# One more tile transposed by DMA, one more reciprocal broadcast by way of DRAM, and late weights issued by GpSimd, in a fused attention and gated-MLP kernel

## The chip, the cores and the metric

One core of one Trainium2 chip. The metric is the device time of one execution in microseconds (us), median of several runs; lower is better. TensorE is called PE, VectorE DVE, ScalarE ACT, GpSimd POOL and SyncE SP.

## The reference

x is 1 x 2048 x 512 in bf16. Two branches work on the layer-normalized x, and their product is added to x:

```python
# A: 32 heads of 16, each position looks at 8 positions, 2 apart, back from itself
q, k, v = split(xn @ wqkv)
logits  = einsum("bhsd,bhswd->bhsw", q, kg) * Dh**-0.5     # kg, vg: k, v gathered at s, s-2, ..., s-14
attn    = softmax(where(mask, logits, -1e9))
s       = einsum("bhsw,bhswd->bhsd", attn, vg) @ wo
# B: gated MLP, 512 -> 1792 -> 512
h = gelu(xn @ w_gate) * (xn @ w_up)
g = silu(h @ w_down)
return x + s * g          # xn = layernorm(x)
```

## The kernel before

It works through the 2048 positions in four chunks of 512 (four tiles of 128 each). For each chunk: 14 "glu" steps (gate and up matmuls, gelu, product), then the q, k and v projections of the next chunk ("qkv"), then 4 "down" steps (w_down, wo, output). The attention of a chunk is laid between these by a table: `at((stage, chunk, step), function, ...)` runs a function ahead of that step. The order of instructions is the order of the program. What the change and the argument touch (cuts are marked):

```python
def load_late_weights():                       # w_down and wo, 5 DMAs on SP's queue
    nc.sync.dma_start(out=wd_sb[:], in_=B_w_down.rearrange("(k p) n -> p k n", p=P))
    for g in range(NC):
        nc.sync.dma_start(out=wo_sb[:, g, :], in_=...)

def moments(t):                                # statistics on DVE, the power -0.5 on POOL
    ...
    nc.gpsimd.tensor_tensor(out=rstd[:, t, :], in0=rstd[:, t, :], in1=mhalf[:], op=ALU.pow)

def transpose(t, parts=1, copy=None):          # 4 PE transposes into a PSUM tile and a copy out of it
    ...
def transpose_by_dma(t):                       # 4 DMA transposes on SP's queue
    ...
def spread_reciprocals(j):                     # 1/denominator to all rows by 4 PE matmuls ("sp_ps") and an ACT copy
    ...
def spread_by_dma(j):                          # the same: stored to DRAM (rs_d), read back four times (rb)
    ...
def av_sums(j):                                # 32 matmuls over the eight products "pv": "o_ps"
    ...
def divide(j):                                 # oT = o_ps * rb, two DVE instructions of 2 groups each
    ...

at(("glu", 0, 7 + i), moments, 2 * TPQ + i)    # i = 0..3: tiles 8 to 11
at(("glu", 0, 8 + i), normalize, 2 * TPQ + i)  # DVE: needs the power
at(("glu", 0, 9), logits, 0)                   # and seven small memsets of E on POOL
...
at(("qkv", 1, 10), av_sums, 0)
at(("glu", 3, 12), spread_reciprocals, 3)      # the last chunk only; the others by DMA
at(("glu", 3, 13), divide, 3)
at(("glu", 0, 0), load_late_weights)
```

The softmax here doesn't subtract the row's maximum and nothing guards it: scores larger than these inputs give would overflow.

## Time and profile before

| | before |
|---|---|
| time, first three runs | 230.54, 231.28 and one of 339.7 us; median 231.28 |
| time, 11 runs of a later session | median 230.46 us (230.14 to 230.93) |
| span in the profile | 228.8 us, mean granted PE clock 1.0 |
| PE busy | 222.7 us, 97% |
| DVE, ACT, POOL busy | 65%, 57%, 10% |
| transfers | mean 106 GB/s |

PE is the bound. A row of a timeline in the profile begins with the start in us, then the length, engine, line, operation, what it writes and reads, and how many instructions stand together; in brackets is how long the engine sat idle before it, and what released it. Ends on PE overlap the next start (the transposes at 22.14 are listed with 0.39 us, and the next group starts at 22.36), so I go by starts.

### The profile page before, as it was taken

How to read it: one execution, taken by the hardware profiler on the slowest of the kernel's cores; microseconds unless marked ns; L12 is line 12 of the kernel's file. 1: busy time of each engine (PE TensorE's matmuls, PEld its weight loads, DVE VectorE, ACT ScalarE, POOL GpSimd, SP SyncE). 2: the span in 40 equal slices, each digit the busy share in tenths (PEclk: the TensorE clock that was granted, in tenths of full speed). 3: DMA queues.
4: the chain of work that ended last, by engine and by line, in shares of the span. 5: the costliest groups of instructions: out<-in, count | busy, mean ns of one | idle time of the engine just before them, and what ended most of it. 6: DMA issues, size and time to landing. Idle time of an engine off the chain costs nothing.

```text
span 228.8 us, 3516 instructions
## 1 busy us (share of the span) xinstructions
PE 222.7 (97%) x1303; PEld 106.8 (47%) x1323; DVE 147.6 (65%) x234; ACT 130.6 (57%) x215; POOL 21.7 (10%) x61
## 2 busy tenths in 40 slices
PE   7999999999999999999999999999999999999994
PEld 5865444444444444444444444444444444444453
DVE  4593996894898198865678169735449429845232
ACT  3679779764514867476721687646741387647211
POOL 1048944100000000110000000000000000000000
PEclk9999999999999999999999999999999999999999
DMA  6999599922366611110266711110038910000001
GB/s 157 357 375 376 140 175 199 315 98 80 91 153 152 135 23 29 27 29 0 92 162 152 162 29 23 26 34 6 30 104 193 202 30 3 0 0 4 23 23 46
DMA packets 29857, 24.33 MB, mean 106 GB/s; under 512 B 9488, under 2 KB 29840, under 8 KB 29840
## 3 DMA queue, kind: packets, MB, share of 16 engines
q1 hardware_dynamic: 29840, 24.11, 41.0%
q8 instruction: 10, 0.16, 0.3%
q14 instruction: 7, 0.06, 0.1%
HBM read 18.61 MB, written 4.31 MB: 100 GB/s over the span
## 4 chain that ended last, share of the span: by engine, by line
PE 94%; ACT 2%; DVE 1%; DMA 1%; issue 1%; ACTq 0%; DVEq 0%
PE y_ps L411 21%; PE u_ps L242 21%; PE g_ps L242 20%; PE qkv_ps L242 17%; PE s_ps L421 6%; PE L_ps L299 3%; PE o_ps L370 3%; DMA x_sb<-in_A_x_dram 1%; PE q_ps L242 1%; PE tr L208 1%; DVE stats L177 1%; ACT L395 1%; ACT u L397 1%; PE den_ps L319 0%; ACT xnT L217 0%
## 5 line engine op out<-in xcount | busy, mean ns | idle before, releaser
L242 PE MATMUL u_ps<-xnT,wu_sb 128*128 128x512 bf16 x223 | 57.3, 379 | 0.2
L242 PE MATMUL g_ps<-xnT,wg_sb 128*128 128x512 bf16 x214 | 56.5, 379 | 0.6 <-issue 0.2
L411 PE MATMUL y_ps<-wd_sb,h 128*128 128x512 bf16 (+1 forms) x234 | 50.9, 366 | 0.2
L399 DVE TENSOR_TENSOR h<-ge,u 128x512 bf16<-128x512 bf16 x56 | 23.8, 424 | 37.5 <-ACT u L397 36.8
L288 DVE TENSOR_TENSOR pk<-q_sb,k_sb 128x2048 bf16<-128x2048 bf16 x32 | 37.8, 1221 | 7.0 <-ACT k_sb L263 7.0
L395 ACT ACTIVATE ge<-g_ps 128x512 bf16<-128x512 f32 x56 | 33.6, 600 | 14.7 <-PE g_ps L242 14.0
L397 ACT ACTIVATE u<-u_ps 128x512 bf16<-128x512 f32 x56 | 33.6, 599 | 14.6 <-PE u_ps L242 14.4
L242 PE MATMUL qkv_ps<-xnT,wqkv_sb 128*128 128x512 bf16 (+1 forms) x203 | 40.5, 354 | 0.2
L356 DVE TENSOR_TENSOR pv<-E,v_arr 128x2048 bf16<-128x2048 bf16 x32 | 38.6, 1217 | 0.0
L411 PEld LDWEIGHTS <-h 128*128 128x128 bf16 x238 | 23.3, 98 | 25.3
L418 ACT ACTIVATE sl<-y_ps 128x512 bf16<-128x512 f32 (+1 forms) x17 | 9.7, 573 | 44.0 <-PE y_ps L411 44.0
L242 PEld LDWEIGHTS <-wu_sb 128*128 128x128 bf16 x224 | 21.9, 98 | 26.6 <-issue 0.3
L242 PEld LDWEIGHTS <-wg_sb 128*128 128x128 bf16 x224 | 21.2, 98 | 26.8 <-issue 3.0
L242 PEld LDWEIGHTS <-wqkv_sb 128*128 128x128 bf16 x224 | 21.7, 98 | 19.6 <-issue 0.4
L429 DVE TENSOR_TENSOR m<-s_ps,sl 128x512 bf16<-128x512 f32 (+1 forms) x17 | 11.2, 658 | 22.4 <-PE s_ps L421 22.4
L421 PE MATMUL s_ps<-wo_sb,oT 128*128 128x512 bf16 (+1 forms) x68 | 16.6, 366 | 0.0
L193 POOL TENSOR_TENSOR rstd<-rstd,mhalf 128x1 f32<-128x1 f32 x12 | 7.7, 638 | 78.9 <-DVE rstd L190 76.7
L266 ACT ACTIVATE vst<-qkv_ps 128x512 bf16<-128x512 f32 x16 | 9.6, 598 | 6.4 <-PE qkv_ps L242 6.4
L263 ACT ACTIVATE k_sb<-qkv_ps 128x512 bf16<-128x512 f32 (+1 forms) x20 | 10.2, 517 | 3.4 <-PE qkv_ps L242 3.2
L260 ACT ACTIVATE q_sb<-qkv_ps 128x512 bf16<-128x512 f32 (+1 forms) x16 | 8.7, 545 | 3.5 <-PE qkv_ps L242 3.3
L421 PEld LDWEIGHTS <-oT 128*128 128x128 bf16 x68 | 6.6, 98 | 7.2
L382 DVE TENSOR_TENSOR oT<-o_ps,rbd 128x1024 bf16<-128x1024 f32 x6 | 7.1, 1219 | 3.7 <-PE qkv_ps L242 3.7
(52 smaller groups left out, 119.3 us busy)
## 6 DMA issues: line engine op xcount, KB each, us to landing
v_arr<-vT SPq DMA_DIRECT2D x16, 520.0 KB, 5.1
vT<-vst SPq DMA_DIRECT2D x16, 128.0 KB, 2.8
out_dram<-o_t SPq DMA_DIRECT2D x15, 128.0 KB, 2.3
wg_sb<-in_B_w_gate_dram SPq DMA_DIRECT2D x2, 896.0 KB, 10.8
wu_sb<-in_B_w_up_dram SPq DMA_DIRECT2D x2, 896.0 KB, 10.9
wd_sb<-in_B_w_down_dram SPq DMA_DIRECT2D x1, 1792.0 KB, 16.9
wqkv_sb<-in_A_wqkv_dram SPq DMA_DIRECT2D x3, 512.0 KB
x_sb<-in_A_x_dram SPq DMA_DIRECT2D x3, 512.0 KB, 11.6
```

Source lines behind the costliest of these rows:

```text
L242: nc.tensor.matmul(ps, lhsT=w[:, dk, lo : lo + P], rhs=xnT[j][:, dk, i0 : i0 + n], start=(dk == 0), stop=(dk == NC - 1),)
L263: nc.scalar.activation(out=k_sb[:, c, lo : lo + n], in_=ps, func=AF.Copy)
L266: nc.scalar.activation(out=vst[:], in_=ps, func=AF.Copy)
L288: nc.vector.tensor_tensor(out=pk[:], in0=st[j]["q"][:], in1=k_sb[:, :, off : off + TQ], op=ALU.mult)
L356: nc.vector.tensor_tensor(out=pv[:], in0=st[j]["E"][:, wh, :].unsqueeze(1).to_broadcast([P, 4, TQ]), in1=st[j]["va"][:, 4 * g : 4 * g + 4, ...
L395: nc.scalar.activation(out=ge[:], in_=g_ps[:], func=AF.Gelu_apprx_tanh)
L397: nc.scalar.activation(out=u[:], in_=u_ps[:], func=AF.Copy)
L399: nc.vector.tensor_tensor(out=h[:], in0=ge[:], in1=u[:], op=ALU.mult)
L411: nc.tensor.matmul(y[:], lhsT=st[j][fc][:, tt * P : (tt + 1) * P], rhs=wd_sb[:, fc, cols], start=(fc == 0), stop=(fc == NF - 1),)
L418: nc.scalar.activation(out=sl[:, cols], in_=y[:], func=AF.Silu)
L421: nc.tensor.matmul(s[:], lhsT=st[j]["oT"][:, g, tt * P : (tt + 1) * P], rhs=wo_sb[:, g, cols], start=(g == 0), stop=(g == NC - 1),)
L429: nc.vector.tensor_tensor(out=m[:], in0=s[:], in1=sl[:, cols], op=ALU.mult)
```

## The change

The intent: PE is the bound, so take four transposes (tile 6) and four spread matmuls (last chunk) off it and let DMAs do the work; take the late weights out of SP's queue, where they now would stand behind more transposes; and bring the first q weights forward. Tile 7 was transposed by DMA before as well; its transposes now stand behind those of tile 6 and behind load_v (the v_arr loads) on SP's queue.

```diff
-    for t in range(TPQ):
+    for t in range(TPQ - 1):
         load_x(t)
-    for i in range(3):
+    load_w(wqkv_sb, A_wqkv, 0, D)
+    load_x(TPQ - 1)
+    for i in range(1, 3):
         load_w(wqkv_sb, A_wqkv, i * D, (i + 1) * D)
...
     def load_late_weights():
-        nc.sync.dma_start(out=wd_sb[:], ...
+        nc.gpsimd.dma_start(out=wd_sb[:], ...
         for g in range(NC):
-            nc.sync.dma_start(
+            nc.gpsimd.dma_start(
...
-        nc.gpsimd.memset(spread[:], 0.0)          # and the 16 copies that fill "spread"
...
-        xn = xns[t] = sm4.tile([P, D], BF16, name="xn")     # 4 buffers, shared with vst and o_t
+        xn = xns[t] = xnp.tile([P, D], BF16, name="xn")     # 6 buffers of its own
...
-        if i < TPQ - 1:
+        if i < 2:
             at(("glu", 0, i), transpose, TPQ + i)
...
-        if j + 1 < NJ:
-            at(("glu", j, 11), spread_by_dma, j)
-            at(("qkv", j + 1, 6), divide, j)
-        else:
-            at(("glu", j, 12), spread_reciprocals, j)       # the PE form is gone
-            at(("glu", j, 13), divide, j)
+        at(("glu", j, 11), spread_reciprocals, j)           # now the DMA form
+        at(("qkv", j + 1, 6) if j + 1 < NJ else ("down", j, 0), divide, j)
...
     warm_up(17, TQ // 2)
+    warm_up(4, P)
...
-    at(("glu", 0, 0), transpose_by_dma, 2 * TPQ - 1)
+    at(("glu", 0, 0), transpose_by_dma, TPQ + 2)
     at(("glu", 0, 0), load_v, 0)
-    at(("glu", 0, 0), load_late_weights)
+    at(("glu", 0, 0), transpose_by_dma, TPQ + 3)
+    at(("glu", 0, 9), load_late_weights)
```

More of the change, by code (lines that the diff above doesn't have):

```diff
@@ L68 @@
     sm4 = pool("sm4", 4)
+    xnp = pool("xnp", 6)
     dram = pool("dram", 1, space=bass.MemoryType.DRAM)
@@ L80 @@
     vT = dram.tile([D, SV], BF16, name="vT")
-    rs_d = [dram.tile([P, P], BF16, name=f"rs_d{j}") for j in range(NJ - 1)]
+    rs_d = [dram.tile([P, P], BF16, name=f"rs_d{j}") for j in range(NJ)]
     def load_x(t, n=1):
@@ L104, in load_late_weights @@
     def load_late_weights():
-        nc.sync.dma_start(out=wd_sb[:], in_=B_w_down.rearrange("(k p) n -> p k n", p=P))
+        nc.gpsimd.dma_start(out=wd_sb[:], in_=B_w_down.rearrange("(k p) n -> p k n", p=P))
         for g in range(NC):
-            nc.sync.dma_start(
+            nc.gpsimd.dma_start(
                 out=wo_sb[:, g, :],
@@ L136 @@
     hsum = const.tile([P, H], BF16, name="hsum")
-    spread = const.tile([P, 4, P], BF16, name="spread")
     dsum = const.tile([P, NC, H], BF16, name="dsum")
@@ L151, in sum_constants @@
             )
-        nc.gpsimd.memset(spread[:], 0.0)
-        for q in range(4):
-            for j in range(4):
-                nc.gpsimd.tensor_copy(
-                    out=spread[H * q : H * (q + 1), q, H * j : H * (j + 1)],
-                    in_=ident[H * q : H * (q + 1), H * q : H * (q + 1)],
-                )
     xnT = {}
@@ L331, in spread_reciprocals @@
     def spread_reciprocals(j):
-        sp = mm.tile([P, TQ], F32, name="sp_ps", tag="mm")
-        for q in range(4):
-            nc.tensor.matmul(
-                sp[:, q * P : (q + 1) * P], lhsT=spread[:, q, :], rhs=st[j]["rs"][:],
-                start=True, stop=True,
-            )
-        rb = op.tile([P, TQ], F32, name="rb")
-        nc.scalar.activation(out=rb[:], in_=sp[:], func=AF.Copy)
-        st[j]["rb"] = rb
-    def spread_by_dma(j):
         nc.sync.dma_start(out=rs_d[j][:, :], in_=st[j]["rs"][:])
-        rb = op.tile([P, TQ], BF16, name="rbd")
+        rb = op.tile([P, TQ], BF16, name="rb")
         for i in range(WL):
@@ L460 @@
     at(("qkv", 1, 3), denominators, 0)
-    at(("qkv", 1, 3), spread_by_dma, 0)
+    at(("qkv", 1, 3), spread_reciprocals, 0)
     at(("qkv", 1, 10), av_sums, 0)
```

## The prediction

> **What bounds the kernel now.** I read the page first (busy times, then the chain that ended last), then the timeline of PE (TensorE), then the same stretches on DVE, POOL, ACT and the SP queue, and last the busy times and DMA rates by window.
>
> ```profile
> span 228.8 us, 3516 instructions
> PE 222.7 (97%) x1303; PEld 106.8 (47%) x1323; DVE 147.6 (65%) x234; ACT 130.6 (57%) x215; POOL 21.7 (10%) x61
> PE 94%; ACT 2%; DVE 1%; DMA 1%; issue 1%; ACTq 0%; DVEq 0%
> ```
>
> PE is busy for 97% of the span and is 94% of the chain. Four 128x512 matmuls follow each other every 0.864 us through almost the whole timeline, which is 216 ns each. So only two things move the time: PE instructions that go away (all of them gain), and new waits of PE. PE is not busy for 6.1 us (228.8 less 222.7), and most of that is the first load and the last store. No rearrangement of transfers in the middle can gain much. It can lose.
>
> The places the change touches, PE first, then DVE and POOL:
>
> ```profile
> 22.14 0.39 PE L208 MATMUL tr<-ident,xn 128*128 128x128 bf16 x4
> 22.36 1.03 PE L242 MATMUL g_ps<-xnT,wg_sb 128*128 128x512 bf16 x4
> ...
> 206.08 0.39 PE L334 MATMUL sp_ps<-rs,spread 128*128 128x128 bf16 x4
> 206.31 1.03 PE L242 MATMUL g_ps<-xnT,wg_sb 128*128 128x512 bf16 x4
> ```
>
> The first pair is the transpose of tile 6, the second the spread of the last chunk's reciprocals. From the start of each to the start of the next group PE advances 0.22 us.
>
> ```profile
> 41.68 0.15 DVE L190 TENSOR_SCALAR rstd<-mv 128x1 f32<-128x1 f32 x1
> 41.75 0.42 DVE L399 TENSOR_TENSOR h<-ge,u 128x512 bf16<-128x512 bf16 x1
> 42.93 0.41 DVE L199 TENSOR_SCALAR xn<-x_sb,mv,rstd 128x512 bf16<-128x512 bf16 x1 [0.76 <-POOL rstd L193]
> ...
> 50.80 3.43 DVE L356 TENSOR_TENSOR pv<-E,v_arr 128x2048 bf16<-128x2048 bf16 x3
> ```
>
> ```profile
> 39.21 0.93 POOL L311 MEMSET E<- 32x2 bf16 x7
> 42.34 0.55 POOL L193 TENSOR_TENSOR rstd<-rstd,mhalf 128x1 f32<-128x1 f32 x1 [2.20 <-DVE h L399]
> ```
>
> This is the sensitive place. DVE already waits 0.76 us for POOL's power of tile 11, and from 42.93 to 54.23 it has no gap. In the changed program's order of instructions the five weight DMAs stand on POOL between these two lines: after the seven E memsets, ahead of the power.
>
> [...]
>
> **The change part by part.**
>
> *Tile 6 by DMA.* Removes four PE transposes, 4 x 55 ns = 0.22 us, all on the path, and one ACT eviction (0.65 us at 23.04), off it. It adds four DMA transposes on SP. Those of one tile took SP 6.09 us at 21.57, then v_arr is issued from 27.83 to 30.48, and tile 7's follow it. v_arr moves at about 195 GB/s until 41 us, when the rate jumps to 323 to 349 GB/s (the windows by microsecond); tile 7's 128 KB lie behind it in the same queue. Estimate: 41 us plus the 2.4 us that a transpose took to land, so 43.5 us. PE needs them at 45.03. Hidden, with about 1.5 us to spare. The six xn buffers keep DVE from waiting.
>
> *Reciprocals of the last chunk by DRAM.* Removes four matmuls, 0.22 us on the path, an ACT copy (0.59 us) off it, and POOL's 16 copies that fill "spread" (8.57 us, off it). The reciprocal ended at 204.48. In the second chunk the store was issued at 97.36, the four reads from 98.82 to 100.56, and a read landed 1.8 us after its issue: about 5 us in all. So rb is there at about 209.5, in time for the divide, which moves anyway: it now stands behind h of the last tile. I put the end of the last u matmul at Y0 (209.76 before, when y starts). u's eviction ends at Y0+0.86, h at Y0+1.33, the two divides (2.35) at Y0+3.68. The s matmuls follow 14 y matmuls, Y0+3.02, and the third needs the second divide: it would start at Y0+3.45 and now starts at about Y0+3.74. Loss 0.3 us. Before, the divide was done at 211.62, which is Y0+1.86.
>
> *Start.* The q weights are issued 0.43 us earlier (one x issue). But q_ps at 7.15 was released by the ACT copy of xnT, 6.71 to 7.10, not by the weights. x tile 3 comes later; its statistics ran at 6.41 and its transposes at 9.55, so half a microsecond of slack or more absorbs it. The four added warm-up matmuls[...] fill 0.43 us of the hole from 4.75 to the first transpose at 5.21. Gain: about 0; I allow 0.2 either way.
>
> *Late weights from GpSimd.* The bytes are no problem. Before, they flowed after v_arr, from 41 to 46.5; now POOL reaches them at 40.14 and y needs wd at 57.7. What counts is T, the time for which the five DMAs hold POOL. The power of tile 11 ends at 40.14 + T + 0.55, and xn of tile 11 starts at 40.74 + T with its handover. From there DVE has 11.30 us without a gap (42.93 to 54.23), so the eighth pv is ready at 52.04 + T. PE's o_ps group begins at 54.09 and needs the eighth pv for its last four of 32 matmuls, at 55.7, or 55.5 with the 0.22 us gained. So PE stalls for max(0, T - 3.45) us. The reciprocal on DVE is late too, but its consumers come later. One more thing in the order listing: the last qkv group ahead of o_ps now waits for DVE, as the buffers turn differently with one tr less; it needs T over about 4 to bind, and then the later wait covers it.
>
> [...] The wd transfer has 128 x 14 rows of 1 KB, wo four times 128. [...]
>
> Sum: -0.22 - 0.22 + 0.3 + 0[...] = +1.7 us. Half a microsecond of that I take off because I may overrate T. On 231.28 that makes about 232.4 us.
>
> **The rivals.**
> 1. *T is short (under 3.5 us).* Then nothing stalls at o_ps and the change is worth -0.15 us, 231.1. [...] Against: five instructions, not one. Chance 0.35.
> 2. *T is long (over 8.3 us).* The stall passes 4.8 us and the kernel is slower by over 2%, 236 or more. For it: 2,304 small rows, and GpSimd's slow small operations (a 32x32 copy took about 0.5 us there). Against: no duration of such a DMA is known here. Chance 0.15.
> 3. *Tile 7's transposes come too late.* The four wo issues behind wd held SP for 14.42 us from 31.24[...]. If transposes are held likewise until 39 us, four issues of 1.3 us and 2.4 us to land make 46.6, a stall of 1.6 us and about 233. It would overlap with the late DVE, which then has time to catch up, so it doesn't simply add. Chance 0.15.
> 4. *The start gains.* Where a run's q weights arrive late, it wins up to 0.43 us: 230.8.
>
> **Range and chances.** Lower end: no stall, a lucky start, a baseline like the fastest run (230.54): 230.4. Upper end: T of about 8 or rival 3 on top of the median: 236.5. Faster by 2% needs 4.6 us, and all idle time of PE is 6.1 us with the first load and last store in it: 0.02. Slower by 2% is rival 2 mostly: 0.16. Within 2%: 0.82.
>
> **What would show each step.** tr groups fall from seven to six and sp_ps is gone: right if g_ps follows without a step of 0.22 us. In the tail, s_ps should split after two matmuls with about 0.3 us idle until DVE's second divide. The POOL queue should show wd and wo from about 40.1; the power of tile 11 should end T later, DVE should sit idle until then, and PE idle ahead of or inside o_ps near 54 us until pv. q_ps should still start within 0.2 us of 7.15. I am wrong if POOL's DMAs return in under 3 us, if the power does not wait behind them, if PE waits at 45 us for xnT, or if y waits for wd near 57.7.

The cuts take a section of rules, a few words in the part on the start and in the first and third rivals, and the working of T, which was the author's estimate and came from no trace, with the stall that followed from it. So the sum lacks a term: with it the sum came to +1.7 us, or 232.4 us after half a microsecond was taken off; the terms that are left, all from the traces, come to -0.14 us.

## The result

The changed kernel is correct and took 231.35 us (median of 6 runs, 231.17 to 231.46); the kernel before, on the same chip, 230.47. The ratio is 1.0033, with a 95% interval of 1.0015 to 1.005: slower by about 0.8 us, and the same by a threshold of 2%. (A ratio here is the mean time of one kernel's runs over that of the other's in the same rounds, so not quite the ratio of the medians that are quoted.) Executions over 1.5% slower than the fastest of the same kernel are left out of the means.

The page of the changed kernel: span, busy time, and the chain of work that ended last.

```profile
span 229.6 us, 3497 instructions
PE 222.6 (97%) x1299; PEld 106.7 (46%) x1319; DVE 148.2 (65%) x234; ACT 129.7 (57%) x213; POOL 16.7 (7%) x49
PE 84%; DVE 6%; POOL 3%; ACT 2%; issue 2%; DVEq 0%; ACTq 0%; POOLq 0%
```

PE's share of the chain fell from 94 to 84%, and DVE and POOL came in with 6 and 3%. A chain like this says that somewhere PE now waits for DVE, and DVE for POOL. It does not say that PE lost 10% of its time: a single short wait is enough to lead the chain over other engines for the whole stretch ahead of it.

The place, in the timelines of the changed kernel, POOL, DVE and PE in turn:

```profile
39.72 1.28 POOL L108 DMA_DIRECT2D wd_sb<-in_B_w_down_dram  x1
41.01 2.73 POOL L110 DMA_DIRECT2D wo_sb<-in_A_wo_dram  x4
43.81 0.56 POOL L188 TENSOR_TENSOR rstd<-rstd,mhalf 128x1 f32<-128x1 f32 x1
```

```profile
44.40 0.41 DVE L194 TENSOR_SCALAR xn<-x_sb,mv,rstd 128x512 bf16<-128x512 bf16 x1 [1.98 <-POOL rstd L188]
...
52.28 3.43 DVE L340 TENSOR_TENSOR pv<-E,v_arr 128x2048 bf16<-128x2048 bf16 x3
```

```profile
53.74 1.70 PE L354 MATMUL o_ps<-pv,hsum 128*32 128x512 bf16 x28
55.76 0.40 PE L354 MATMUL o_ps<-pv,hsum 128*32 128x512 bf16 x4 [0.33 <-DVE pv L340]
56.10 1.90 PE L237 MATMUL qkv_ps<-xnT,wqkv_sb 128*128 128x512 bf16 x7
```

The five DMAs hold POOL from 39.72 to 43.74, so T is 4.02 us. The power of tile 11 stands right behind them, DVE waits 1.98 us for it (0.76 before), and the last product pv ends at 55.71 (54.23 before). PE has done 28 of its 32 o_ps matmuls by then and waits. The same place on PE in the kernel before:

```profile
54.09 1.91 PE L370 MATMUL o_ps<-pv,hsum 128*32 128x512 bf16 x32
55.93 1.90 PE L242 MATMUL qkv_ps<-xnT,wqkv_sb 128*128 128x512 bf16 x7
```

Undisturbed, the next qkv group starts 1.84 us after o_ps starts; in the changed kernel it is 2.36. The stall is 0.52 us.

The two places where PE instructions went away, PE's timeline of the changed kernel:

```profile
21.16 1.02 PE L237 MATMUL u_ps<-xnT,wu_sb 128*128 128x512 bf16 x4
22.02 1.03 PE L237 MATMUL g_ps<-xnT,wg_sb 128*128 128x512 bf16 x4
...
205.38 1.03 PE L237 MATMUL u_ps<-xnT,wu_sb 128*128 128x512 bf16 x4
206.25 1.03 PE L237 MATMUL g_ps<-xnT,wg_sb 128*128 128x512 bf16 x4
```

From u_ps to g_ps PE now takes 0.86 and 0.87 us; with the transposes (tr) and the spread (sp_ps) between them it took 1.08 and 1.09 before. That is 0.22 us each.

The tail, PE's timeline of the kernel before and then of the changed kernel:

```profile
209.76 3.19 PE L411 MATMUL y_ps<-wd_sb,h 128*128 128x512 bf16 x14
212.78 1.03 PE L421 MATMUL s_ps<-wo_sb,oT 128*128 128x512 bf16 x4
213.64 3.19 PE L411 MATMUL y_ps<-wd_sb,h 128*128 128x512 bf16 x13
```

```profile
209.70 3.19 PE L395 MATMUL y_ps<-wd_sb,h 128*128 128x512 bf16 x14
212.72 1.22 PE L405 MATMUL s_ps<-wo_sb,oT 128*128 128x512 bf16 x4
213.78 3.19 PE L395 MATMUL y_ps<-wd_sb,h 128*128 128x512 bf16 x13
```

The s group takes 1.22 rather than 1.03 us: within it PE waits for the second divide, which ended at 213.28. The loss from s to the next y is 0.20 us (1.06 against 0.86).

From the last o_t on DVE to the end of the program: 2.42 us before, 3.10 after. These are the instructions of the program's end, gathered by their source line, before and then after (count, then min/median/max in ns, first and last start); what is said below of single ones among them was read from the packed trace, which has each one's start:

```profile
L558 SPq EVENT_SEMAPHORE  x8: 17/28/28, 226.8 to 228.7; - x8
L558 POOLq EVENT_SEMAPHORE_RANGE_CLEAR  x1: 96/96/96, 228.4 to 228.4; - x1
```

```profile
L540 SPq EVENT_SEMAPHORE  x10: 17/28/28, 226.9 to 229.5; - x10
L540 POOLq EVENT_SEMAPHORE_RANGE_CLEAR  x1: 139/139/139, 228.8 to 228.8; - x1
```

The steps of the difference, all from starts in the two traces:

| step | us |
|---|---|
| start: q_ps at 7.15 before, 7.03 after; 0.11 of it left at the first g_ps (18.25 and 18.14) | -0.1 |
| tile 6 transposed by DMA (third g_ps: 22.36 and 22.02) | -0.22 |
| stall inside o_ps | +0.52 |
| spread matmuls gone | -0.22 |
| s group waits for the second divide | +0.20 |
| sum up to the last o_t (226.37 before, 226.50 after) | +0.13 measured, +0.18 by the terms |
| from the last o_t to the end of the program | +0.68 |
| span | +0.8 |

So the two gains on PE came in full, two waits of 0.72 us together more than ate them, and most of what is left of the 0.8 us is at the very end, behind all work.

### The profile page after: what moved, and what is told of

It is laid out like the page before. It is cut to its first block, busy times and chain, and to the rows that moved or that the text cites. A ratio compares the mean times of both kernels' runs of the same rounds, so it can differ in the third digit from the quotient of the medians.

```text
span 229.6 us, 3497 instructions
## 1 busy us (share of the span) xinstructions
PE 222.6 (97%) x1299; PEld 106.7 (46%) x1319; DVE 148.2 (65%) x234; ACT 129.7 (57%) x213; POOL 16.7 (7%) x49
## 4 chain that ended last, share of the span: by engine, by line
PE 84%; DVE 6%; POOL 3%; ACT 2%; issue 2%; DVEq 0%; ACTq 0%; POOLq 0%
PE y_ps L395 21%; PE u_ps L237 18%; PE g_ps L237 17%; PE qkv_ps L237 14%; PE s_ps L405 6%; DVE pv L340 4%; PE o_ps L354 2%; PE L_ps L294 2%; PE warm_ps L220 2%; POOL rstd L188 1%; POOL wo_sb L110 1%; PE q_ps L237 1%; ACT u L381 1%; DVE h L383 1%; ACT L379 1%
## 5 line engine op out<-in xcount | busy, mean ns | idle before, releaser
L413 DVE TENSOR_TENSOR m<-s_ps,sl 128x512 bf16<-128x512 f32 (+1 forms) x17 | 11.2, 657 | 21.3 <-PE s_ps L405 21.3
L366 DVE TENSOR_TENSOR oT<-o_ps,rb 128x1024 bf16<-128x1024 f32 x8 | 9.4, 1218 | 2.2 <-DMA rb<-rs_d 2.2
```

What stands on the lines that cost most here:

```text
L413: nc.vector.tensor_tensor(out=m[:], in0=s[:], in1=sl[:, cols], op=ALU.mult)
```

## The experiments

Theory after the result: the loss is a sum of three things, (1) the stall at o_ps, through POOL's hold T, as max(0, T - 3.45); (2) the late last divide, 0.2 us; (3) the longer end of the program. Rivals: the bytes of the late weights, now moved at another time, cost something by themselves; the start costs or gains; DMAs on GpSimd lengthen the end of any program. All runs were correct. The kernel before had medians of 230.46 (two sessions, the first eight runs) and 230.49 us (the last four); the edits are against the changed kernel unless the text says otherwise.

**Late weights back on SP.**

```diff
-        nc.gpsimd.dma_start(out=wd_sb[:], ...        # and the four of wo
+        nc.sync.dma_start(out=wd_sb[:], ...
-    at(("glu", 0, 9), load_late_weights)
+    at(("glu", 0, 0), load_late_weights)
```

> The changed kernel with the late weights back on the SP queue (behind the transposes of tile 7); the rest of the change stays. My theory: of the 0.9 us lost against the kernel before, 0.5 us is PE waiting inside the first o_ps group for pv, because POOL's power of tile 11 stands behind five DMAs that hold POOL for 4.0 us, and some 0.4 us is the end of the program, where a handshake of GpSimd took 0.45 us instead of 0.08. So both go: no idle in o_ps, about 230.4 us, equal to the kernel before within 0.2 us. Rival (the late reciprocal or a slower DMA makes pv late, and the end is longer for another reason): stall and time stay, about 231.3.

Measured: 230.52 us (230.11 to 230.82), ratio 1.0002 (0.9989 to 1.0014). PE's timeline:

```profile
53.31 1.91 PE L354 MATMUL o_ps<-pv,hsum 128*32 128x512 bf16 x32
```

o_ps is one group of 32 again, without a wait. This one edit returns the whole loss: it removes the stall and shortens the end (2.57 us from the last o_t). All other parts of the change together are worth nothing measurable.

**Late weights behind the power.** They stay on GpSimd, two steps later, behind the power of tile 11.

```diff
-    at(("glu", 0, 9), load_late_weights)
+    at(("glu", 0, 11), load_late_weights)
```

> The changed kernel with the late weights still from GpSimd's queue but two tiles later, so that the power of tile 11 is ahead of them on POOL. My theory: the 2 us that DVE waits before xn of tile 11 and the 0.33 us gap inside o_ps go, the end of the program stays long: about 230.85 us, half a microsecond under the changed kernel. If wd or wo came too late, y near 57.5 us or the first s would wait instead. Rival (the GpSimd queue's traffic, not the order on POOL, delays pv): no change, 231.35.

Measured: 231.25 us (230.92 to 231.56), ratio 1.0038. A miss. PE's timeline, then a line of DVE's:

```profile
53.52 1.91 PE L354 MATMUL o_ps<-pv,hsum 128*32 128x512 bf16 x32
...
60.12 0.60 PE L405 MATMUL s_ps<-wo_sb,oT 128*128 128x512 bf16 x2
61.18 0.60 PE L405 MATMUL s_ps<-wo_sb,oT 128*128 128x512 bf16 x2 [0.47 <-DVE oT L366]
```

```profile
58.77 2.35 DVE L366 TENSOR_TENSOR oT<-o_ps,rb 128x1024 bf16<-128x1024 f32 x2 [5.38 <-DMA rb<-rs_d]
```

The stall at o_ps is gone, as theory (1) wants. A new one stands at s_ps, 0.65 us by starts (1.51 us from s to the next y, 0.86 undisturbed): DVE gets the reciprocals, on their way through DRAM, at 58.77, which is 0.84 us later than in the changed kernel (57.93). (That it waits 5.38 us for them and not 2.22 overstates this, as it began to wait 2.3 us earlier.) What lags is the store to DRAM: SP issues it at 50.07 and the reads behind it at 54.80, 4.73 us later; in the changed kernel it is 52.39 and 53.91, 1.52 us. In that time the weights' bytes flow, from 45 to 53 us, at 301 to 345 GB/s up to 51. So the rival about the bytes fits here: when a transfer starts matters, not only who issues it. No run tests it apart. With the late weights on SP the reads also came 4.06 us behind the store, and there it cost PE nothing.

**Last divide back ahead of the last glu step.**

```diff
-        at(("qkv", j + 1, 6) if j + 1 < NJ else ("down", j, 0), divide, j)
+        at(("qkv", j + 1, 6) if j + 1 < NJ else ("glu", j, 13), divide, j)
```

> The changed kernel with the last chunk's divide put back ahead of the last h on DVE, the reciprocals still by way of DRAM. My theory: the last chunk's first s_ps group (1.22 us long instead of 1.03) loses 0.19 us to the second divide; that goes, about 231.15 us. Rival: rb lands too late for the earlier place (it was issued to 207.92 and should land near 209.7), DVE then holds the last h and y waits for it, 231.35 or more.

Measured: 230.82 us (230.71 to 231.08), ratio 1.002. PE's timeline:

```profile
212.37 1.03 PE L405 MATMUL s_ps<-wo_sb,oT 128*128 128x512 bf16 x4
213.23 3.18 PE L395 MATMUL y_ps<-wd_sb,h 128*128 128x512 bf16 x14
```

s takes 1.03 us again, and the next y follows after 0.86: the 0.2 us are the divide's. The median fell by more (0.53). In the profiled run q_ps started at 6.60 rather than 7.03, so a good part of the rest is the start, which varies from run to run (PE's first four transposes took 0.40 us here and 0.61 in the changed kernel). The o_ps stall stays (0.32 us of idle time).

**Four more stores on SP**, to a scratch tensor, so that the semaphore of the last output store is one that SP checks last.

```diff
+    def dummies():
+        for i in range(4):
+            nc.sync.dma_start(out=scr[:, 4 * i : 4 * i + 4], in_=warm[:, 4 * i : 4 * i + 4])
+    at(("qkv", 2, 0), dummies)
```

> The changed kernel with four tiny stores of no use on the SP queue at about 101 us, where SP is idle. Nothing waits for them; they turn the semaphore lanes of the DMAs by four, so that the last output store takes the lane that SP checks last at the end of the program instead of the fourth of eight. My theory: after the last store has landed SP has one check left and not five, 4 x 0.06 us = 0.24 us less, about 231.1 us. Rival: the checks after the landing cost nothing or the order is another: 231.35.

Measured: 231.02 us (230.93 to 231.19), ratio 1.0026. From the last o_t to the end 2.83 us rather than 3.10. At the end SP checks the semaphores of the DMAs one after the other, about 0.06 us each (in the changed kernel three from 226.91 on, the fourth when the last store has landed, at 228.09, and four more to 228.33); the last store lands 1.22 us after its issue ends, in the kernel before and in the changed one. If its semaphore is the fourth in the row, four more checks follow the landing; here none does. That is worth the 0.27 us.

**One small DMA from GpSimd at the start**, in the kernel before.

```diff
+    nc.gpsimd.dma_start(out=scr[:, 0:4], in_=warm[:, 0:4])     # against the kernel before
```

> The kernel before with one DMA of 1 KB from GpSimd's queue at its start, to a DRAM tile that nothing reads; nothing waits for it and the number of SP's DMAs is the same. My theory: a program that uses GpSimd's DMA queue at all ends later: the gap between GpSimd's last two semaphore instructions goes from 0.08 to 0.45 us as in the changed kernel, so about 230.85 us against 230.46. Rival: the 0.45 us comes with the five DMAs' semaphores or with the layout of the changed program; then 230.5.

Measured: 231.58 us (231.08 to 233.16), ratio 1.0038. A miss, and not for the reason under test: the gap between GpSimd's last two semaphore instructions stayed at 0.078 us, so using GpSimd's queue is not what widens it. The time went at the other end:

```profile
8.38 3.29 PE L244 MATMUL q_ps<-xnT,wqkv_sb 128*128 128x256 bf16 x16 [2.15 <-DMA wqkv_sb<-in_A_wqkv_dram]
```

In the profiled run, which was the slowest of the six, q_ps waited 2.15 us for its weights and then ran at half speed (16 matmuls in 3.13 us to the next start; 1.74 us in the kernel before). The granted clock in the trace is 0.50 from 7.9 to 11.2 us. Whether the 1 KB DMA delays those weights, and how, is not settled; the other runs of it have no trace.

**Late weights from GpSimd alone**, in the kernel before.

```diff
-            nc.sync.dma_start(           # wd and wo, against the kernel before
+            nc.gpsimd.dma_start(
-    at(("glu", 0, 0), load_late_weights)
+    at(("glu", 0, 9), load_late_weights)
```

> The kernel before with that part of the change alone: late weights from GpSimd's queue after the E memsets of tile 9. My theory: POOL reaches them at 40.1 us and is held 4.0 us, the eighth pv is ready at 56.1 instead of 54.2 and o_ps needs it at 55.7: a stall of 0.36 us, less than in the changed kernel (0.52) because PE has not gained the 0.22 us of tile 6 and comes later. The end of the program grows by 0.44 us (GpSimd's handshake and the longer clearing of semaphores) and by about 0.3 us for the last store's lane, third of eight. Together about 231.5 us. Rival: the loss in the changed kernel needs the other parts too (transposes of tile 7 behind v_arr): then under 231.0.

Measured: 231.42 us (231.16 to 232.0), ratio 1.0044. PE's timeline:

```profile
55.89 0.40 PE L370 MATMUL o_ps<-pv,hsum 128*32 128x512 bf16 x4 [0.32 <-DVE pv L356]
```

This one part, done alone, makes the stall (0.50 us by starts, 53.88 to 56.22; expected were 0.36) and lengthens the end (2.80 us rather than 2.42). Its loss is about that of the whole change, though not made of the same parts: the gains on PE and the late divide are missing, and of the end only the checks and the longer clear are here, not the gap of GpSimd (0.078 us; the expectation had counted on it). That the two totals agree is in part chance. With the first experiment it shows the stall from both sides.

**The start undone.**

```diff
-    warm_up(4, P)                              # the added warm-up
...
-    load_w(wqkv_sb, A_wqkv, 0, D)              # and x tile 3 ahead of the q weights again
-    load_x(TPQ - 1)
```

> The changed kernel with the start of the kernel before: x tile 3 ahead of the q weights, no extra warm-up matmuls. My theory: the start is worth about nothing, as the first projection is released by the ACT copy of xnT or at nearly the same time by the q weights[...]: 231.35 within 0.2 us. Rival: the q weights bound the start[...] (two profiles here show q_ps waiting for them by 0.3 to 0.4 us), so undoing it costs up to 0.4: 231.7.

Measured: 231.41 us (231.11 to 231.84), ratio 1.004. The start is worth nothing that shows: 0.06 us from the changed kernel.

**A version without the three losses.** Late weights on SP, the divide early, and x tiles 8 to 15 in one load, so that the last store's semaphore is checked last.

```diff
-    at(("glu", 0, 9), load_late_weights)       # with the queues as in the first experiment
+    at(("glu", 0, 0), load_late_weights)
...
-        at(("qkv", j + 1, 6) if j + 1 < NJ else ("down", j, 0), divide, j)
+        at(("qkv", j + 1, 6) if j + 1 < NJ else ("glu", j, 13), divide, j)
...
-        load_x((2 + i) * TPQ, TPQ)
+        if i == 1:
+            load_x(2 * TPQ, 2 * TPQ)
```

> The parts that only remove PE work: tile 6 and 7 by DMA, last reciprocals by way of DRAM, q weights early, but late weights on SP's queue, the last divide ahead of the last h, and two x loads made one so that the last store takes the lane that is checked last. My theory: against the kernel before only the 0.22 us of tile 6 and the 0.22 us of the spread remain, no stall in o_ps or s_ps and the end as before: 230.0 us, 0.2% faster than before (230.46). Rival (PE is held elsewhere and the removed groups only give back slack): 230.4.

Measured: 230.24 us (229.73 to 230.87), ratio 0.999 (0.9976 to 1.0004). No stall is left, and the end takes 2.40 us. It is the fastest median of all, but its interval holds 1: the 0.44 us of PE work that the change takes away is no more than the runs of one kernel differ among themselves. In the profiled runs it can be seen: the last o_t ends at 225.96, before at 226.37, though q_ps had started no earlier (7.19 and 7.15).

**POOL held twice as long.** wd in seven DMAs rather than one, with the same bytes.

```diff
-        nc.gpsimd.dma_start(out=wd_sb[:], in_=B_w_down.rearrange("(k p) n -> p k n", p=P))
+        for k in range(0, NF, 2):
+            nc.gpsimd.dma_start(out=wd_sb[:, k : k + 2, :], in_=...[:, k : k + 2, :])
```

> The changed kernel with the wd load cut into seven DMAs of 256 rows on GpSimd, eleven in all. From 1.28 us for 1792 rows and 0.68 for 128 an estimate of 0.63 us for each DMA and 0.36 ns for each row follows, so T should be about 7.8 us. Theory (the prediction's formula): PE then stalls ahead of the last pv's matmuls for T - 3.45 = 4.3 us rather than 0.52, and the time is about 235.2. Rival 1 (the cost goes with the rows, not with the DMAs): T stays near 4 us, time 231.4. Rival 2 (a later slack swallows a part or another wait adds): T is 7.8 but the time is not between 234.5 and 236.

Measured: 235.38 us (235.17 to 235.59), ratio 1.021 (1.0188 to 1.0232). POOL's timeline and then PE's:

```profile
39.29 5.26 POOL L109 DMA_DIRECT2D wd_sb<-in_B_w_down_dram  x7
44.55 2.79 POOL L114 DMA_DIRECT2D wo_sb<-in_A_wo_dram  x4
47.41 0.56 POOL L192 TENSOR_TENSOR rstd<-rstd,mhalf 128x1 f32<-128x1 f32 x1
```

```profile
56.02 1.87 PE L241 MATMUL qkv_ps<-xnT,wqkv_sb 128*128 128x512 bf16 x4 [3.52 <-DVE rs L327]
57.82 2.54 PE L358 MATMUL o_ps<-pv,hsum 128*32 128x512 bf16 x32
60.29 1.90 PE L241 MATMUL qkv_ps<-xnT,wqkv_sb 128*128 128x512 bf16 x7
```

The seven DMAs of wd take 5.26 us (0.75 each) where one took 1.28, for the same 1792 rows. A wo part of 128 rows takes 0.68, the 1 KB DMA above took 0.72. So the cost goes with the number of DMAs and hardly with the rows, and T is 8.05 us. The formula gives a stall of 4.6. To set the run against the changed kernel, take the qkv group behind o_ps: it starts 4.19 us later (60.29 against 56.10), though q_ps had started 0.44 us earlier (6.59 against 7.03). That is 4.63 us more than the 0.52 there, so about 5.15 in all. The size is 12% over the formula's, but the way is another. PE waits for the qkv group's PSUM buffer, which DVE's reciprocal frees (3.52 us), and then runs at half speed (the granted clock in the trace is 0.50 from 55.8 to 59.1 us): four qkv matmuls take 1.80 us rather than 0.86, and o_ps 2.47 rather than 1.84, which is 1.57 us more. For pv it does not wait at all. The last pv ends at 59.32, and PE, being slow, comes to the last four o_ps matmuls only at 59.98. At full clock it would have come to them at about 58.5 and waited some 0.8 us, 4.3 in all (an estimate from these numbers). So the run shows that POOL's hold reaches PE through DVE and grows with T; it does not confirm the formula's own wait at this size. By the threshold of 2% the run is undecided (its interval holds 1.02); slower than the changed kernel it clearly is.

**Late weights when GpSimd has nothing to do**, from 20.9 us on.

```diff
-    at(("glu", 0, 9), load_late_weights)
+    at(("glu", 0, 0), load_late_weights)        # still on GpSimd
```

> The changed kernel with its late weights on GpSimd but at the first gate tile, where GpSimd has nothing to do from 20.6 to 33 us. The hold of POOL then costs nothing, so no stall by the power of tile 11: 230.85 if the bytes disturb nothing. Rival: the 2.3 MB now flow ahead of v_arr and of the last x and up weights, which come later, and PE waits for pv or x: 231.5 to 234. End gap: 0.44 by theory A (69 records again).

Measured: 240.01 us (238.93 to 240.79), ratio 1.0407. The rival was right, and by more than I had put. PE's and DVE's timelines:

```profile
50.41 4.88 PE L237 MATMUL qkv_ps<-xnT,wqkv_sb 128*128 128x512 bf16 x11 [6.00 <-DMA xnT<-xn]
```

```profile
50.19 1.23 DVE L340 TENSOR_TENSOR pv<-E,v_arr 128x2048 bf16<-128x2048 bf16 x1 [7.62 <-DMA v_arr<-vT]
```

The DMA engines are busy all the time from 16 to 48 us in this run (the share that the view gives is 1.01 or more in each stretch of 4 us; in the changed kernel it is 0.37 and 0.61 in the two from 24 to 32); the weights take their place between 24 and 32 us (271 to 309 GB/s; 95 to 134 in the changed kernel), v_arr and the transposes of tile 7 come late, and PE stands still for 6.0 us at the first qkv step of the second chunk and then runs at half speed (5.23 us to the start of den_ps, 2.68 in the changed kernel; the granted clock is 0.50 from 50.4 to 55.6 us). This is the outcome that the prediction's third rival names, tile 7 too late, though with the weights' bytes ahead of it, where the prediction had put it down to the wo issues on SP: a transpose landed as late as 16.1 us after its issue here, 11.8 in the changed kernel. The gap at the end is 0.434 us, as the expectation had it. So freeing POOL's hold from the path is not enough: the place that costs POOL nothing is the worst one for the transfers.

**The end of the program, two more tests.** The gap of 0.45 us between GpSimd's last two semaphore instructions stood, by then, in every variant with 69 recorded GpSimd instructions and in none with 64, 81, 82 or 86. So the first test adds five memsets to the kernel with late weights on SP; the second keeps the 17 GpSimd instructions that fill the unused matrix "spread" in the changed kernel.

```diff
+    five = const.tile([P, 40], BF16, name="five")        # first test
+    at(("glu", 0, 9), five_memsets)                      # 5 x nc.gpsimd.memset(five[:, 8*i : 8*i+8], 0.0)
```

```diff
+        nc.gpsimd.memset(spread[:], 0.0)                 # second test, and its 16 copies
```

> The changed kernel with its late weights back on SP (230.52 in the earlier run) plus five small memsets on GpSimd at the place where the five DMAs stood, so that GpSimd has as many records (69) as in the changed kernel but issues no DMA. Theory A (the 0.37 us between GpSimd's last two semaphore instructions comes from where its instructions end, since so far all kernels with 69 records have it and those with 64, 81, 82 and 86 have not): the gap is 0.44 us, RANGE_CLEAR stays at 96 ns, time 230.9. Theory B (it comes from five DMAs on GpSimd together with something else of the change): the gap stays 0.078 and the time 230.5.

> The changed kernel with the 17 GpSimd instructions that fill the unused spread matrix kept (86 records, five DMAs). Theory A (place of the end): the gap is 0.078 and the time 231.0, while RANGE_CLEAR stays near 140 ns because GpSimd still issues DMAs. Theory B: the gap stays 0.44 and the time 231.35. Either way the stall ahead of the last four o_ps matmuls stays near 0.3 to 0.5 us.

Measured: 230.73 us (230.3 to 231.39), ratio 1.0006, gap 0.079 us. The gap did not come, but neither did the test reach what theory A asks for: the trace has 68 recorded GpSimd instructions and not 69 (five memsets more than with the late weights on SP, and one semaphore instruction fewer), so it does not refute A. And 230.9 us (230.58 to 231.49), ratio 1.0018 (0.9998 to 1.0037), gap 0.078 us: theory A right, with five DMAs on GpSimd in place and the o_ps stall still there (0.34 us of idle time). The end of the program in the kernels that tell something, from their traces:

| kernel | DMAs from GpSimd | last o_t to end, us | checks behind the landing | RANGE_CLEAR, ns | gap between the last two, us |
|---|---|---|---|---|---|
| before | 0 | 2.42 | 0 | 96 | 0.078 |
| changed | 5 | 3.10 | 4 | 139 | 0.447 |
| late weights on SP | 0 | 2.57 | 2 | 96 | 0.078 |
| the same and five memsets | 0 | 2.58 | 2 | 96 | 0.079 |
| four more stores | 5 | 2.83 | 0 | 142 | 0.446 |
| before, one small GpSimd DMA | 1 | 2.48 | 0 | 142 | 0.078 |
| before, late weights from GpSimd | 5 | 2.80 | 5 | 142 | 0.078 |
| spread fill kept | 5 | 2.72 | 4 | 139 | 0.078 |
| wd in seven | 11 | 2.73 | 4 | 142 | 0.078 |

What is shown: the order of the checks (0.06 us each), and the longer clear when GpSimd has issued any DMA at all (about 45 ns). Of the gap it is shown that neither the use of GpSimd's queue nor the number of its DMAs makes it (1, 5 and 11 DMAs have been seen without it), and that 17 GpSimd instructions early in the program take it away. In all traces kept, every kernel with 69 recorded GpSimd instructions has the gap (0.434 to 0.454 us in six kernels) and none with 64, 68, 75, 81, 82 or 86. That fits a dependence on where GpSimd's instructions end, but no run brought the gap about on purpose. Its cause stays open. It is worth 0.37 us.

## Why the prediction was wrong, point by point

- **The failed step: T.** The prediction's hold of POOL was the estimate, which no trace showed. Measured are 4.02 us (0.68 for each wo part, 1.28 for wd) and 0.52. The formula T - 3.45 was close: with the true T it gives 0.57. (In the other run of this size, late weights from GpSimd alone, the expectation worked out in the same way was 0.36 and 0.50 were measured, so it is good to some 0.15 us.) But a stall that is what remains above a slack of 3.45 us magnifies an error: the measured T was 24% under the estimate, and the stall 3.6 times smaller than the forecast one. With 4.02 in place of the estimate the prediction's own sum, without its hedge of half a microsecond, falls from +1.7 to +0.4 us. The run with eleven DMAs lost 5.15 us for the formula's 4.6: the path from POOL over DVE to PE carries to twice the T, but there the wait for the reciprocal and the slower clock made the loss, not the wait for pv.
- **A step that was missing: the end of the program,** +0.68 us, nearly all of the loss in the span. Nothing in the prediction looked behind the last store. It came from which semaphore the last store has (about 0.27 us), from a longer clear (0.04), and from a gap that is not explained (0.37).
- **The level.** The forecast started from 231.28, the median of three runs of which one was an outlier; eleven later runs have 230.46. So 0.8 of the 1.05 us between the forecast of 232.4 and the measured 231.35 is the level. As a change the forecast was +1.1 us on its own level and the measurement +0.8 to 0.9; that these come near each other is because the overrated stall, the half microsecond taken off and the missing end nearly cancel, not because the steps were right: that is luck.
- **Right: the two gains on PE,** 0.22 us each, to the hundredth, as steps from u_ps to g_ps at 22 and at 206 us.
- **Right: the last divide,** 0.3 us put, 0.20 measured, and confirmed by moving it back. DVE's second divide ended 3.58 us after y starts and not 3.68. The group did not show as split in the timeline, as the prediction had said it would; it only got longer.
- **Right: the start,** about 0; undone, it changed the time by 0.06 us.
- **The rivals.** The short T (under 3.5) and the long one (over 8.3) did not happen; T lay half a microsecond above the first. The late transposes did not happen either: PE took up qkv at 44.69 without a wait. The prediction said that the wait for the PSUM buffer "needs T over about 4 to bind, and then the later wait covers it". At T = 4.02 it didn't bind; at 8.05 it did, and no later wait covered it, as PE ran at half speed after it and found pv ready. Nor does the fourth show, that an earlier issue of the q weights gains up to 0.43 us: with the start undone the time is 231.41.
- **What the intent missed.** The change takes 0.44 us from PE and gives back 0.72 in two waits, each set by an order: POOL's power behind five DMAs, and the divide behind the last h. Late weights from GpSimd do not help PE at any of the three places tried.

## What to carry to other kernels

A DMA moved to another engine's queue is first an instruction in that engine's order (five of them held GpSimd for 4.02 us here): find what stands behind it and how much slack the engine that waits for it has, and give the loss as hold less slack, with a range, because a small error in the hold is a large one in the difference. Then ask when the bytes will flow: the same weights, moved a few microseconds earlier or later, made PE wait 6 us for a transpose or half a microsecond for a reciprocal. In a kernel whose bound engine is 97% busy, gains of 0.2 us must be weighed against the last store's place in the semaphore checks (0.27 us here) and the spread of the runs (230.14 to 230.93 us in 11 runs of the kernel before).
